# The last part's r and k products in float16 pairs, with scales found on the chip

## The chip, the cores and the metric

The kernel runs on one NeuronCore of one Trainium2 chip. The metric is the device time of the whole launch in microseconds (us), lower is better. Five engines matter: PE (matrix products, with its weight loads shown as PEld), DVE (vector work), ACT (activation functions and copies), POOL (vector work on a slower engine, reductions across partitions) and SP (which issues the DMA transfers). Each takes its own instructions in the order in which the compiled program lists them, and waits at an instruction until what it reads is there.

## The reference

Linear attention on 8 batches of 576 positions, then a feed-forward net behind a Fourier transform, then a gated net (the last part). Only the last part is touched by the change:

```python
def _moe2_ref(x, mu_k, mu_r, w_k, w_v, w_r):
    x_prev = x shifted by one position, zeros at the start of each batch
    xk = mu_k * x + (1.0 - mu_k) * x_prev
    xr = mu_r * x + (1.0 - mu_r) * x_prev
    k = np.maximum(xk @ w_k, 0.0)          # 512 -> 1024
    v = k * k @ w_v                        # 1024 -> 512
    r = 1.0 / (1.0 + np.exp(-(xr @ w_r)))  # 512 -> 512
    return r * v
```

The weights arrive as 64-bit floats. The kernel gets a float32 out of each pair of words on the chip.

## The kernel before

Tokens (8 x 576 = 4608) are cut into 9 blocks of 512. The program has three stretches.

The front (attention, Fourier transform, normalisation, lines 314 to 660) runs as generators `front_x` and `front_y`. The feed-forward main loop (lines 823 to 887) calls them piece by piece through `side()`, four times in each step of a block, so that the front of the later batches lies beside the products of the earlier ones. In the main loop a block has 16 steps; each is 12 products of 512 columns at L846 (first layer, into the PSUM tile `h`) and 12 at L866 (second layer, into four accumulators `acc`), all float16: a float32 number is held as a high and a low float16 part and three products stand for one. ACT writes the high part of the result (`hh`, L851) and DVE the low part (`hl`, L852), two steps ahead of their use.

The last strand (`last_strand`, L804) is called through the same `side()` when the front is used up. It first runs `last_weights` (L668): for each chunk of 128 x 256 weights a DMA into one of three `raw` buffers (L150), three DVE instructions that make a float32 from the two words (L157 to L159), an ACT copy into the high part (L684) and a DVE subtraction for the low part (L685). There are 8 chunks of `w_r`, 16 of `w_k` and 16 of `w_v`, in this order. Then it loads the block's activations (`load_y`) and mixes them (`mix`, L701): per quarter of the features an ACT product (L714), a POOL memset of one column where a batch starts (L717), a DVE multiply-add (L718), an ACT copy to the high part (L719), a DVE subtraction for the low part (L720). For the second and later blocks `mix` is called from the last part's own loop.

The last part (lines 890 to 956) takes the 9 blocks in turn. A block has 48 products for r (L908, four groups of 12, sigmoid by ACT at L909), 96 for k (L919, `mmk`, eight groups of 12), and 96 for v (L934, `mmv`). All three use float32r, a format of 4 bytes, again in high and low parts. Behind each `mmk` ACT takes relu (L923), DVE multiplies by it once more (L924, so k squared), ACT copies the high part (L925) and DVE subtracts (L926). `mmv(f)` uses what `mmk(f)` left two groups earlier. Two PSUM tiles `h` alternate, so `mmk(f+2)` waits until L924 has read the tile of `mmk(f)`.

The compiled order of the instructions is not the order of the source: when the program is built, a planner simulates the engines and moves an instruction forward where its engine would be idle. So the chunks of `last_weights`, which the source places in block 7 of the main loop, run from the end of block 6 on.

Of the kernel before, what the change touches and what calls it, by code (L numbers as in the profile page):

```python
# [22 lines left out]
RAW = 3  # L23
# [18 lines left out]
LEAST = (1.0 + 0x300000 / 2.0 ** 23) * 2.0 ** (0x73 - 127)  # L42
# [3 lines left out]
def net(ctx, tc, q, k, v, w1, w2, mu_k, mu_r, w_k, w_v, w_r, ce_d, se_d, cs_d, ss_d, alt_d, id_d, out):  # L46
    nc = tc.nc
# [4 lines left out]
    FK = w_k.shape[1]  # L52
    NFK = FK // 128
    blocks = [(t, min(512, NT - t)) for t in range(0, NT, 512)]
# [6 lines left out]
    def bank(tag, bufs, shape=(128, 512)):  # L61
        return ps.tile(list(shape), F32, tag=tag, name=tag, bufs=bufs)
# [27 lines left out]
    up = main.enter_context(tc.tile_pool(name="up", bufs=4, side="right"))  # L90
    hp = main.enter_context(tc.tile_pool(name="hp", bufs=1, side="right"))
# [107 lines left out]
    def scales(w):  # L199
# [66 lines left out]
    W = {}  # L266
# [37 lines left out]
    def attention(b):  # L304
        tt = nc.vector.tensor_tensor
        for hf in range(2):
# [14 lines left out]
            m = fw.tile([128, 4, 64], F32, tag="m", name="m")  # L321
            nc.vector.tensor_reduce(out=m, in_=kc.rearrange("p c h d -> p h d c"), axis=AX.X, op=ALU.max)  # L322
            for x in range(2):
                p = slice(64 * x, 64 * x + 64)
                tt(out=m[p, 2 * x:2 * x + 2, :], in0=m[p, 2 * x:2 * x + 2, :], in1=kt[p, 16:18, :], op=ALU.max)
            if b in MAX_PE:
# [4 lines left out]
                mx = wsc[:, 2:6:3, None]  # L331
                nc.vector.tensor_reduce(out=mx[:, :, 0], in_=pt[:, 0:256].rearrange("p (x c) -> p x c", x=2), axis=AX.X, op=ALU.max)
                dg = m.rearrange("p h d -> p (h d)").rearrange("p (x c) -> p x c", x=2)
# [7 lines left out]
            st = fw.tile([128, 2, 18, 1], F32, tag="st", name="st")  # L341
            nc.vector.tensor_reduce(out=st[:, 0, :, 0], in_=qt, axis=AX.X, op=ALU.max)
            beside = nc.gpsimd.tensor_tensor if (b, hf) in POOL_Q else tt
# [322 lines left out]


    back_pools = ExitStack()  # L668
    def last_weights():

        wp = W["pool"] = back_pools.enter_context(tc.tile_pool(name="wp", bufs=1))
        W["mu"] = wp.tile([128, 2, 2, 4], F32, name="mu")
        for x, src in enumerate((mu_k, mu_r)):
            nc.sync.dma_start(out=W["mu"][:, x, 0, :], in_=src)
        nc.vector.tensor_scalar(out=W["mu"][:, :, 1], in0=W["mu"][:, :, 0], scalar1=-1.0, scalar2=1.0, op0=ALU.mult, op1=ALU.add)
        for name, src, nt, n in (("wr", w_r, 4, DM), ("wk", w_k, 4, FK), ("wv", w_v, NFK, DM)):
            h = wp.tile([128, nt, n], F32R, name=name + "h")
            l = wp.tile([128, nt, n], F32R, name=name + "l")
            W[name] = h, l
            for t in range(nt):  # L680
                for c in range(n // 256):
                    cs = slice(256 * c, 256 * c + 256)
                    x = decode(wp, load_weight(wp, src, t, c, RAW))
                    nc.scalar.activation(out=h[:, t, cs], in_=x, func=AF.Copy)  # L684
                    nc.vector.tensor_tensor(out=l[:, t, cs], in0=x, in1=h[:, t, cs].bitcast(F32), op=ALU.subtract)  # L685
                    yield 0


    Y = {}
    X = {}  # L690

    def load_y(i):
        t0, n = blocks[i]
# [4 lines left out]
        else:  # L698
            nc.sync.dma_start(out=y[:, :, 0:n + 1], in_=yT[:, :, t0 - 1:t0 + n].rearrange("t p n -> p t n"))

    def mix(i, w):  # L701

        t0, n = blocks[i]
        y = Y[i]
        mu = W["mu"]
        if w == 1:
            h, l = (up.tile([128, 4, 512], F32R, tag="u", name="x") for _ in range(2))
        else:
            h, l = (hp.tile([128, 4, 512], F32R, tag=x, name="x") for x in ("sq", "d"))
        X[i, w] = h, l  # L710
        aa = hp.tile([128, 2, 512], F32, tag="rs", name="aa")
        for t in range(4):
            a = aa[:, t % 2, 0:n]
            nc.scalar.activation(out=a, in_=y[:, t, 0:n], func=AF.Copy, scale=mu[:, w, 1, t:t + 1])  # L714
            for b, s, m, o in segments(i):
                if s == 0:
                    nc.gpsimd.memset(a[:, o:o + 1], 0.0)  # L717
            nc.vector.scalar_tensor_tensor(out=a, in0=y[:, t, 1:n + 1], scalar=mu[:, w, 0, t:t + 1], in1=a, op0=ALU.mult, op1=ALU.add)  # L718
            nc.scalar.activation(out=h[:, t, 0:n], in_=a, func=AF.Copy)  # L719
            nc.vector.tensor_tensor(out=l[:, t, 0:n], in0=a, in1=h[:, t, 0:n].bitcast(F32), op=ALU.subtract)  # L720
            yield 0


# [164 lines left out]
        side()  # L888


    mu = W["mu"]
    (wkh, wkl), (wvh, wvl), (wrh, wrl) = W["wk"], W["wv"], W["wr"]
    kk = big.tile([128, 2, 4, 512], F32R, tag="w1h", name="kk")
    ke = big.tile([128, 8, 512], F32, tag="w1l", name="ke")
# [2 lines left out]
    for i, (t0, n) in enumerate(blocks):  # L897
        subs = [(o, min(128, n - o)) for o in range(0, n, 128)]
        rh, rl = X.pop((i, 1))
        kh, kl = X.pop((i, 0))  # L900
        acc = [bank(f"acc{x}", 1) for x in range(4)]
        E = ke[:, 0:4, :]
        nxt = iter(())
        for x, (o, m) in enumerate(subs):
            pt = bank("h", 2)
            for t in range(4):
                for a, c in ((rh, wrh), (rh, wrl), (rl, wrh)):
                    mm(out=pt[0:m, :], lhsT=a[:, t, o:o + m], rhs=c[:, t, :], start=(t == 0 and a is rh and c is wrh), stop=(t == 3 and a is rl))  # L908
            nc.scalar.activation(out=E[0:m, x, :], in_=pt[0:m, :], func=AF.Sigmoid)  # L909
        if i + 1 < NB:  # L910
            nxt = mix(i + 1, 1)
        K2 = {}

        def mmk(f):
            pt = bank("h", 2)
            fs = slice(128 * f, 128 * f + 128)
            for t in range(4):
                for a, c in ((wkh, kh), (wkh, kl), (wkl, kh)):
                    mm(out=pt[:, 0:n], lhsT=a[:, t, fs], rhs=c[:, t, 0:n], start=(t == 0 and a is wkh and c is kh), stop=(t == 3 and a is wkl))  # L919
            kr = ke[:, 4 + count[0] % 4, :]  # L920
            h2, l2 = kk[:, 0, count[0] % 4, :], kk[:, 1, count[0] % 4, :]
            count[0] += 1
            nc.scalar.activation(out=kr[:, 0:n], in_=pt[:, 0:n], func=AF.Relu)  # L923
            nc.vector.scalar_tensor_tensor(out=kr[:, 0:n], in0=pt[:, 0:n], scalar=0.0, in1=kr[:, 0:n], op0=ALU.max, op1=ALU.mult)  # L924
            nc.scalar.activation(out=h2[:, 0:n], in_=kr[:, 0:n], func=AF.Copy)  # L925
            nc.vector.tensor_tensor(out=l2[:, 0:n], in0=kr[:, 0:n], in1=h2[:, 0:n].bitcast(F32), op=ALU.subtract)  # L926
            K2[f] = h2, l2

        def mmv(*fs):
            for x, (o, m) in enumerate(subs):  # L930
                for f in fs:
                    h2, l2 = K2[f]
                    for a, c in ((h2, wvh), (h2, wvl), (l2, wvh)):
                        mm(out=acc[x][0:m, :], lhsT=a[:, o:o + m], rhs=c[:, f, :], start=(f == 0 and a is h2 and c is wvh), stop=(f == NFK - 1 and a is l2))  # L934


        lag = 3 if i == NB - 1 else 2
# [131 lines left out]
```

## Time and profile before

| what | value |
|---|---|
| median of three runs | 1605.52 us (1602.82 to 1607.69) |
| the profiled execution's own time | 1604.72 us |
| its span, first to last instruction | 1602.9 us |
| mean granted TensorE clock, as a share of full speed | 0.971 |
| PE busy / PEld busy | 93% / 59% |
| DVE / ACT / POOL busy | 56% / 36% / 10% |

The time of an execution is 1.8 us more than its span. PE's busy share counts modelled ends of pipelined products, so the distance between the starts of successive products says more than a product's duration.

### The profile page before, as it was taken

Reading aid. Unit: us, or ns where it says so; the run is one execution under the profiler, and the core shown is the slowest. Engines: PE = TensorE matmul, PEld = TensorE weight load, DVE = VectorE, ACT = ScalarE, POOL = GpSimd, SP = SyncE. Lnnn points to the kernel's source line nnn. Section 1 sums busy time; section 2 is a strip of 40 time slices with the busy share of each in tenths; the row PEclk is TensorE's granted clock in tenths of the full one; section 3 lists DMA queues with packets and bytes.
Section 4 is the critical chain, followed back from the end, with each engine's and each line's share of the span. In section 5 each row is a group of like instructions: output and inputs, shape, how many; then the busy total and the mean of one; then the engine's idle time right before and its main releaser. Section 6 shows DMA issues by size and latency. Waiting matters only on the chain.

```text
span 1602.9 us, 17944 instructions
## 1 busy us (share of the span) xinstructions
PE 1489.3 (93%) x7072; PEld 945.5 (59%) x7072; DVE 893.8 (56%) x1496; ACT 579.1 (36%) x1010; POOL 164.8 (10%) x174
## 2 busy tenths in 40 slices
PE   4657895899999999999999899999999999999999
PEld 3535443555555555555555344446888888888887
DVE  6899958646657465485454893513344443434432
ACT  4655543333234233242232331313334433433421
POOL 0034422120010110110200210000000000000000
PEclk9778997899999999999999999999999999999999
DMA  9845411101111012021011330101001101100000
GB/s 356 315 134 181 147 58 72 47 32 46 42 46 59 15 47 73 1 73 47 0 53 47 99 119 27 54 0 53 27 27 53 53 16 37 53 27 27 27 27 27
DMA packets 41407, 105.98 MB, mean 66 GB/s; under 512 B 5323, under 2 KB 11628, under 8 KB 40300
## 3 DMA queue, kind: packets, MB, share of 16 engines
q1 hardware_dynamic: 41324, 104.85, 18.6%
q8 instruction: 55, 0.90, 0.2%
q14 instruction: 28, 0.23, 0.0%
HBM read 85.96 MB, written 18.87 MB: 65 GB/s over the span
## 4 chain that ended last, share of the span: by engine, by line
PE 78%; DVE 14%; DMA 3%; issue 2%; ACT 2%; POOL 1%; SPq 0%; DVEq 0%; POOLq 0%; ACTq 0%
PE acc L866 18%; PE h L846 18%; PE acc L934 13%; PE h L919 13%; PE h L908 6%; PE side L495 2%; PE side L515 2%; DMA raw<-in_w_k_dram 1%; PE side L416 1%; PE side L363 1%; DMA raw<-in_w_dram 1%; DVE words L239 1%; DVE m L322 1%; DVE top L197 1%; DVE eo L450 1%
## 5 line engine op out<-in xcount | busy, mean ns | idle before, releaser
L846 PE MATMUL h<-unh,w1h 128*128 128x512 f16 (+1 forms) x608 | 225.3, 371 | 7.3 <-DVE hl L852 4.2
L846 PE MATMUL h<-unh,w1l 128*128 128x512 f16 (+1 forms) x608 | 223.9, 370 | 5.5 <-POOL w1l L257 5.5
L846 PE MATMUL h<-unl,w1h 128*128 128x512 f16 (+1 forms) x608 | 225.0, 370 | 1.2 <-DVE unl L658 1.2
L866 PE MATMUL acc<-hl,w2h 128*128 128x512 f16 x576 | 219.8, 382 | 2.7 <-DVE hl L852 2.7
L866 PE MATMUL acc<-hh,w2l 128*128 128x512 f16 x576 | 219.9, 382 | 0.0
L866 PE MATMUL acc<-hh,w2h 128*128 128x512 f16 x576 | 211.7, 381 | 4.9 <-ACT hh L851 4.9
L846 PEld LDWEIGHTS <-w1h 128*128 128x128 f16 x1216 | 118.3, 99 | 136.8 <-issue 7.8
L852 DVE SCALAR_TENSOR_TENSOR hl<-h,hh 128x512 f16<-128x512 f32 x144 | 98.9, 688 | 179.5 <-ACT hh L851 178.6
L866 PEld LDWEIGHTS <-w2h 128*128 128x128 f16 x1152 | 111.8, 98 | 137.0 <-issue 8.1
L934 PE MATMUL acc<-wvh,kk 128*128 128x512 f32 x576 | 190.6, 395 | 0.0
L919 PE MATMUL h<-x,wkh 128*128 128x512 f32 x576 | 180.8, 395 | 0.0
L851 ACT ACTIVATE hh<-h 128x512 f16<-128x512 f32 x144 | 85.0, 592 | 215.4 <-PE h L846 215.2
L924 DVE SCALAR_TENSOR_TENSOR ke<-h,ke 128x512 f32<-128x512 f32 x72 | 49.7, 690 | 177.5 <-ACT ke L923 177.4
L934 PEld LDWEIGHTS acc<-wvh,kk 128*128 128x128 f32 x576 | 108.1, 188 | 26.3
L919 PEld LDWEIGHTS h<-x,wkh 128*128 128x128 f32 x576 | 108.1, 188 | 26.2
L934 PE MATMUL acc<-wvl,kk 128*128 128x512 f32 x288 | 113.7, 395 | 0.0
L919 PE MATMUL h<-x,wkl 128*128 128x512 f32 x288 | 113.7, 395 | 0.0
L923 ACT ACTIVATE ke<-h 128x512 f32<-128x512 f32 x72 | 42.9, 596 | 175.6 <-PE h L919 175.5
L846 PEld LDWEIGHTS <-w1l 128*128 128x128 f16 x608 | 59.7, 98 | 72.4 <-POOL w1l L257 7.9
L866 PEld LDWEIGHTS <-w2l 128*128 128x128 f16 x576 | 56.6, 98 | 67.5 <-issue 5.3
L908 PE MATMUL h<-wrh,x 128*128 128x512 f32 x288 | 92.1, 396 | 0.0
L720 DVE TENSOR_TENSOR x<-aa,x 128x512 fp32r<-128x512 f32 x72 | 47.8, 688 | 72.6 <-PE h L908 62.4
(309 smaller groups left out, 2253.3 us busy)
## 6 DMA issues: line engine op xcount, KB each, us to landing
raw<-in_w_dram SPq DMA_DIRECT2D x22, 512.0 KB, 3.8
vt<-in_v_dram SPq DMA_DIRECT2D x16, 650.0 KB, 5.2
kt<-in_k_dram SPq DMA_DIRECT2D x16, 576.0 KB, 3.9
qt<-in_q_dram SPq DMA_DIRECT2D x16, 576.0 KB, 4.0
out_dram<-oo SPq DMA_DIRECT2D x36, 256.0 KB, 2.1
y<-yT SPq DMA_DIRECT2D x8, 1026.0 KB, 5.1
w2h<-in_w_dram SPq DMA_DIRECT2D x8, 1024.0 KB, 5.1
w2l<-in_w_dram SPq DMA_DIRECT2D x8, 1024.0 KB, 7.1
```

Of the source, the lines that this page charges most:

```text
L495: mm(out=pt, lhsT=a[:, e, g, js], rhs=c[:, g, :], start=first, stop=(e == 1 and g == 1 and a is el))
L515: mm(out=pt, lhsT=a[:, i, cols], rhs=c[:, i, :], start=(i == 0 and c is ch and a is yh), stop=False)
L720: nc.vector.tensor_tensor(out=l[:, t, 0:n], in0=a, in1=h[:, t, 0:n].bitcast(F32), op=ALU.subtract)
L846: mm(out=pt[:, o:o + m], lhsT=a[:, t, fs], rhs=c[:, t, o:o + m], start=(t == 0 and a is w1h and c is xh), stop=(t == 3 and a is w1l))
L851: nc.scalar.activation(out=hh[:, 0:n], in_=pt[:, 0:n], func=AF.Relu)
L852: nc.vector.scalar_tensor_tensor(out=hl[:, 0:n], in0=pt[:, 0:n], scalar=0.0, in1=hh[:, 0:n], op0=ALU.max, op1=ALU.subtract)
L866: mm(out=acc[x][:, 0:n], lhsT=a[:, f, xs], rhs=c[:, 0:n], start=(f == 0 and a is w2h and c is hh), stop=(f == NF - 1 and a is w2l))
L908: mm(out=pt[0:m, :], lhsT=a[:, t, o:o + m], rhs=c[:, t, :], start=(t == 0 and a is rh and c is wrh), stop=(t == 3 and a is rl))
L919: mm(out=pt[:, 0:n], lhsT=a[:, t, fs], rhs=c[:, t, 0:n], start=(t == 0 and a is wkh and c is kh), stop=(t == 3 and a is wkl))
L923: nc.scalar.activation(out=kr[:, 0:n], in_=pt[:, 0:n], func=AF.Relu)
L924: nc.vector.scalar_tensor_tensor(out=kr[:, 0:n], in0=pt[:, 0:n], scalar=0.0, in1=kr[:, 0:n], op0=ALU.max, op1=ALU.mult)
L934: mm(out=acc[x][0:m, :], lhsT=a[:, o:o + m], rhs=c[:, f, :], start=(f == 0 and a is h2 and c is wvh), stop=(f == NFK - 1 and a is l2))
```

## The change

`last_weights` first finds two bounds. For `w_r` and `w_k` (24 chunks) it loads each chunk, takes the absolute value of the words' upper 16 bits by ACT into a bfloat16 tile, and the maximum by DVE; then the maximum across partitions by POOL. From this come powers of two. Only then are the weights loaded (again, for `w_r` and `w_k`) and cut, in the order `w_v`, `w_r`, `w_k`; r's and k's are scaled and held as two float16 parts, v's stay float32r. For each block of tokens `bound` finds the largest absolute value of the block (a DVE reduction over 4 x 513 numbers per partition, then POOL across partitions), and six small DVE instructions make the block's scales. The mixing factors carry the scale, the mixed activations are float16 pairs, and the sigmoid and the relu undo the scales through their scale operand. The memset at batch starts goes from POOL to DVE. The number of products, their shapes and their order are the same.

```diff
+        top = wp.tile([128, 4], F32, name="top")
+        am = wp.tile([128, 2, 16], F32, name="am")
+        nc.gpsimd.memset(am, 0.0)
...
+        for w, (name, src, nt, n) in enumerate(plan[0:2]):
+            for t in range(nt):
+                for c in range(n // 256):
+                    raw = load_weight(wp, src, t, c, RAW)
+                    hw = wp.tile([128, 256], BF16, tag="hw", name="hw", bufs=2)
+                    a = t * (n // 256) + c
+                    nc.scalar.activation(out=hw, in_=raw[:, :, 1:2].bitcast(BF16)[:, :, 1], func=AF.Abs)
+                    ts(out=hw, in0=hw, scalar1=0.0, scalar2=None, op0=ALU.max, op1=ALU.max, accum_out=am[:, w, a:a + 1])
+                    yield 0
+        nc.vector.tensor_reduce(out=top[:, 0:2], in_=am, axis=AX.X, op=ALU.max)
+        nc.gpsimd.partition_all_reduce(out_ap=top[:, 0:3], in_ap=top[:, 0:3], channels=128, reduce_op=bass_isa.ReduceOp.max)
...
+        for name, src, nt, n in (plan[2], plan[0], plan[1]):
+            f16 = name != "wv"
...
+            h = wp.tile([128, nt, n], F16 if f16 else F32R, name=name + "h")
+            l = wp.tile([128, nt, n], F16 if f16 else F32R, name=name + "l")
...
+                    if f16:
+                        s = pw[:, 2 + (name == "wk"):3 + (name == "wk")]
+                        nc.scalar.activation(out=h[:, t, cs], in_=x, func=AF.Copy, scale=s)
+                        nc.vector.scalar_tensor_tensor(out=l[:, t, cs], in0=x, scalar=s, in1=h[:, t, cs], op0=ALU.mult, op1=ALU.subtract)
...
+    def bound(i):
...
+        nc.vector.tensor_reduce(out=z[:, 0:1], in_=Y[i][:, :, 0:n + 1], axis=AX.XY, op=ALU.max, apply_absolute_value=True)
+        nc.gpsimd.partition_all_reduce(out_ap=z[:, 0:1], in_ap=z[:, 0:1], channels=128, reduce_op=bass_isa.ReduceOp.max)
+        yield 0
+        zi = z.bitcast(U32)
+        ts(out=z[:, 1:2], in0=z[:, 0:1], scalar1=W["top"][:, 2:3], scalar2=LEAST, op0=ALU.mult, op1=ALU.max)
...
     def mix(i, w):
...
+        if i not in SC:
+            yield from bound(i)
+        mu = SC[i][1]
         if w == 1:
-            h, l = (up.tile([128, 4, 512], F32R, tag="u", name="x") for _ in range(2))
+            h, l = (up.tile([128, 4, 512], F16, tag="u", name="x") for _ in range(2))
...
-                    nc.gpsimd.memset(a[:, o:o + 1], 0.0)
+                    nc.vector.memset(a[:, o:o + 1], 0.0)
...
-            nc.scalar.activation(out=E[0:m, x, :], in_=pt[0:m, :], func=AF.Sigmoid)
+            nc.scalar.activation(out=E[0:m, x, :], in_=pt[0:m, :], func=AF.Sigmoid, scale=z[0:m, 3:4])
...
-            nc.scalar.activation(out=kr[:, 0:n], in_=pt[:, 0:n], func=AF.Relu)
+            nc.scalar.activation(out=kr[:, 0:n], in_=pt[:, 0:n], func=AF.Relu, scale=z[:, 5:6])
```

## Rows read from the trace of the kernel before

**Rows 1.** Busy by stretch: length, each engine's busy us (instructions), granted clock, DMA.

```profile
880.00:940.00 60.00, 51.69 (x220) 22.23 (x218) 54.22 (x115) 19.73 (x42) 14.83 (x6) 0.94 0.34 108
867.00:972.00 105.00, 96.69 (x428) 42.64 (x426) 93.28 (x212) 37.03 (x77) 16.29 (x9) 0.97 0.35 111
972.00:1095.00 123.00, 123.00 (x572) 55.73 (x570) 33.91 (x54) 25.75 (x42) 0.79 (x8) 1.00 0.05 18
1095.00:1603.00 508.00, 504.15 (x2163) 405.39 (x2161) 204.60 (x309) 184.56 (x306) 5.32 (x54) 1.00 0.10 36
```

**Rows 2.** The chain that ended last: start us, us, engine, tile, line, products.

```profile
1004.87 7.77 PE acc L866 x36
...
1095.51 11.19 PE h L908 x48
1106.71 8.40 PE h L919 x36
```

**Rows 3.** A group of PE: count, busy us, mean ns of one, idle before.

```profile
L919 PE MATMUL h<-x,wkh 128*128 128x512 f32 x576 | 180.8, 395 | 0.0
```

**Rows 4.** Whom PE waited for, 820 to 1000 us: total us, times, longest.

```profile
PE acc L866 <- ACT hh L851: 4.5, 2, 2.5
PE acc L866 <- DVE hl L852: 2.7, 2, 2.3
```

**Rows 5.** ACT in order of time, before PE's longest wait (914.6).

```profile
913.67 0.42 ACT L684 ACTIVATE wkh<-dec 128x256 fp32r<-128x256 f32 x1 [2.92 <-DVE dec L159]
913.99 0.58 ACT L851 ACTIVATE hh<-h 128x512 f16<-128x512 f32 x1
```

**Rows 6.** PE in order of time, a float32r product among float16 ones.

```profile
941.84 0.38 PE L846 MATMUL h<-unl,w1h 128*128 128x512 f16 x1
941.87 0.58 PE L581 MATMUL side<-hl,onesr 128*128 128x512 f32 x1
942.29 0.39 PE L846 MATMUL h<-unh,w1l 128*128 128x512 f16 x1
```

**Rows 7.** Groups that cut the weights (L158), and searched the main loop's (L196, L197).

```profile
L158 DVE SCALAR_TENSOR_TENSOR dec<-raw,dec 128x256 uint32<-128x256 uint32 x40 | 19.5, 494 | 0.1
...
L197 DVE TENSOR_SCALAR_CACHE_REDUCE top<-top 128x512 bf16<-128x512 bf16 x32 | 20.6, 680 | 0.2
...
L197 DVE DVE_READ_ACCUMULATOR top<-top 128x1 f32 x32 | 2.6, 82 | 0.0
...
L196 ACT ACTIVATE top<-w2l 128x512 bf16<-128x512 bf16 x16 | 9.7, 650 | 0.0
```

**Rows 8.** DMA issues: count, KB each, median us from issue to landing.

```profile
raw<-in_w_k_dram SPq DMA_DIRECT2D x16, 256.0 KB, 3.2
```

**Rows 9.** DVE in order of time: the last weight chunk, then block 0's mixing.

```profile
971.51 0.43 DVE L685 TENSOR_TENSOR wvl<-dec,wvh 128x256 fp32r<-128x256 f32 x1 [0.48 <-ACT wvh L684]
...
1017.33 1.29 DVE L720 TENSOR_TENSOR x<-aa,x 128x512 fp32r<-128x512 f32 x2 [0.74 <-DMA yT<-u]
...
1034.44 1.41 DVE L718 SCALAR_TENSOR_TENSOR aa<-y,mu,aa 128x512 f32<-128x512 f32 x2 [2.32 <-POOL aa L717]
```

**Rows 10.** POOL in order of time: two of the ten maxima across partitions.

```profile
262.69 1.08 POOL L338 PARTITION_ALL_REDUCE m<-m  x1 [6.02 <-issue]
...
739.85 1.06 POOL L338 PARTITION_ALL_REDUCE m<-m  x1 [23.62 <-DVE m L325]
```

**Rows 11.** Groups nearest to the added instructions, and the mixing lines.

```profile
L718 DVE SCALAR_TENSOR_TENSOR aa<-y,mu,aa 128x512 f32<-128x512 f32 x72 | 51.0, 747 | 15.2 <-POOL aa L717 14.2 <-ACT aa L714 1.0
...
L322 DVE TENSOR_REDUCE m<-kt 128x256 f32<-128x1024 f32 x16 | 31.0, 1936 | 11.9 <-DMA kt<-in_k_dram 11.8
L354 DVE TENSOR_REDUCE st<-qt 128x18 f32<-128x1152 f32 x16 | 21.6, 1351 | 11.8 <-ACT qt L345 11.8
...
L458 DVE MEMSET eo<- 1x289 f32 x3 | 0.9, 299 | 0.0
...
L714 ACT ACTIVATE aa<-y,mu 128x512 f32<-128x512 f32 x72 | 48.2, 716 | 13.9 <-DVE x L720 7.8 <-DVE d L644 3.9 <-DMA y<-yT 2.1
```

More of the change, by code (lines that the diff above doesn't have):

```diff
@@ L671, in last_weights @@
         wp = W["pool"] = back_pools.enter_context(tc.tile_pool(name="wp", bufs=1))
+        ts = nc.vector.tensor_scalar
         W["mu"] = wp.tile([128, 2, 2, 4], F32, name="mu")
@@ L674, in last_weights @@
             nc.sync.dma_start(out=W["mu"][:, x, 0, :], in_=src)
[L675 to L678, printed above, removed]
+        ts(out=W["mu"][:, :, 1], in0=W["mu"][:, :, 0], scalar1=-1.0, scalar2=1.0, op0=ALU.mult, op1=ALU.add)
@@ new lines, in last_weights @@
+        top = wp.tile([128, 4], F32, name="top")
+        am = wp.tile([128, 2, 16], F32, name="am")
+        nc.gpsimd.memset(am, 0.0)
+        ab = wp.tile([128, 2, 2, 4], F32, name="ab")
+        nc.vector.scalar_tensor_tensor(out=ab, in0=W["mu"], scalar=-1.0, in1=W["mu"], op0=ALU.mult, op1=ALU.max)
+        nc.vector.tensor_tensor(out=ab[:, :, 0], in0=ab[:, :, 0], in1=ab[:, :, 1], op=ALU.add)
+        nc.vector.tensor_reduce(out=top[:, 2:3], in_=ab[:, :, 0], axis=AX.XY, op=ALU.max)
+        yield 0
@@ new lines, in last_weights @@
+        plan = (("wr", w_r, 4, DM), ("wk", w_k, 4, FK), ("wv", w_v, NFK, DM))
+        for w, (name, src, nt, n) in enumerate(plan[0:2]):
[7 more added lines that the diff above has]
+                    yield 0
@@ new lines, in last_weights @@
+        nc.vector.tensor_reduce(out=top[:, 0:2], in_=am, axis=AX.X, op=ALU.max)
+        nc.gpsimd.partition_all_reduce(out_ap=top[:, 0:3], in_ap=top[:, 0:3], channels=128, reduce_op=bass_isa.ReduceOp.max)
+        yield 0
+        W["top"] = top
+        pw = W["pw"] = wp.tile([128, 4], F32, name="pw")
+        scaled = False
+        for name, src, nt, n in (plan[2], plan[0], plan[1]):
+            f16 = name != "wv"
+            if f16 and not scaled:
+                m, inv, big_ = pw[:, 0:2], pw[:, 2:4], top[:, 0:2]
+                mi, ii, bi = m.bitcast(U32), inv.bitcast(U32), big_.bitcast(U32)
+                ts(out=big_, in0=big_, scalar1=LEAST, scalar2=None, op0=ALU.max)
+                ts(out=mi, in0=bi, scalar1=3, scalar2=0x3F800000, op0=ALU.logical_shift_left, op1=ALU.bitwise_and)
+                nc.vector.scalar_tensor_tensor(out=mi, in0=bi, scalar=0x40000000, in1=mi, op0=ALU.bitwise_and, op1=ALU.bitwise_or)
+                ts(out=ii, in0=mi, scalar1=0x7F800000, scalar2=None, op0=ALU.bitwise_xor)
+                ts(out=inv, in0=inv, scalar1=2.0 ** 11, scalar2=None, op0=ALU.mult)
+                scaled = True
+            h = wp.tile([128, nt, n], F16 if f16 else F32R, name=name + "h")
+            l = wp.tile([128, nt, n], F16 if f16 else F32R, name=name + "l")
@@ L683, in last_weights @@
                     x = decode(wp, load_weight(wp, src, t, c, RAW))
-                    nc.scalar.activation(out=h[:, t, cs], in_=x, func=AF.Copy)
-                    nc.vector.tensor_tensor(out=l[:, t, cs], in0=x, in1=h[:, t, cs].bitcast(F32), op=ALU.subtract)
+                    if f16:
+                        s = pw[:, 2 + (name == "wk"):3 + (name == "wk")]
+                        nc.scalar.activation(out=h[:, t, cs], in_=x, func=AF.Copy, scale=s)
+                        nc.vector.scalar_tensor_tensor(out=l[:, t, cs], in0=x, scalar=s, in1=h[:, t, cs], op0=ALU.mult, op1=ALU.subtract)
+                    else:
+                        nc.scalar.activation(out=h[:, t, cs], in_=x, func=AF.Copy)
+                        nc.vector.tensor_tensor(out=l[:, t, cs], in0=x, in1=h[:, t, cs].bitcast(F32), op=ALU.subtract)
                     yield 0
@@ L690, in net @@
     X = {}
+    SC = {}
     def load_y(i):
@@ L699, in load_y @@
             nc.sync.dma_start(out=y[:, :, 0:n + 1], in_=yT[:, :, t0 - 1:t0 + n].rearrange("t p n -> p t n"))
+    def bound(i):
+        n = blocks[i][1]
+        ts = nc.vector.tensor_scalar
+        z = W["pool"].tile([128, 6], F32, tag="z", name="z", bufs=3)
+        ms = W["pool"].tile([128, 2, 2, 4], F32, tag="ms", name="ms", bufs=3)
+        SC[i] = z, ms
+        nc.vector.tensor_reduce(out=z[:, 0:1], in_=Y[i][:, :, 0:n + 1], axis=AX.XY, op=ALU.max, apply_absolute_value=True)
+        nc.gpsimd.partition_all_reduce(out_ap=z[:, 0:1], in_ap=z[:, 0:1], channels=128, reduce_op=bass_isa.ReduceOp.max)
+        yield 0
+        zi = z.bitcast(U32)
+        ts(out=z[:, 1:2], in0=z[:, 0:1], scalar1=W["top"][:, 2:3], scalar2=LEAST, op0=ALU.mult, op1=ALU.max)
+        ts(out=zi[:, 1:2], in0=zi[:, 1:2], scalar1=0x7F800000, scalar2=None, op0=ALU.bitwise_and)
+        ts(out=zi[:, 2:3], in0=zi[:, 1:2], scalar1=0x7F800000, scalar2=None, op0=ALU.bitwise_xor)
+        ts(out=ms, in0=W["mu"], scalar1=z[:, 2:3], scalar2=2.0 ** 12, op0=ALU.mult, op1=ALU.mult)
+        ts(out=z[:, 3:5], in0=W["pw"][:, 0:2], scalar1=z[:, 1:2], scalar2=2.0 ** -25, op0=ALU.mult, op1=ALU.mult)
+        nc.vector.tensor_tensor(out=z[:, 5:6], in0=z[:, 4:5], in1=z[:, 4:5], op=ALU.mult)
+        yield 0
     def mix(i, w):
@@ L704, in mix @@
         y = Y[i]
-        mu = W["mu"]
+        if i not in SC:
+            yield from bound(i)
+        mu = SC[i][1]
         if w == 1:
-            h, l = (up.tile([128, 4, 512], F32R, tag="u", name="x") for _ in range(2))
+            h, l = (up.tile([128, 4, 512], F16, tag="u", name="x") for _ in range(2))
         else:
-            h, l = (hp.tile([128, 4, 512], F32R, tag=x, name="x") for x in ("sq", "d"))
+            h, l = (hp.tile([128, 4, 512], F16, tag=x, name="x") for x in ("sq", "d"))
         X[i, w] = h, l
@@ L716, in mix @@
                 if s == 0:
-                    nc.gpsimd.memset(a[:, o:o + 1], 0.0)
+                    nc.vector.memset(a[:, o:o + 1], 0.0)
             nc.vector.scalar_tensor_tensor(out=a, in0=y[:, t, 1:n + 1], scalar=mu[:, w, 0, t:t + 1], in1=a, op0=ALU.mult, op1=ALU.add)
             nc.scalar.activation(out=h[:, t, 0:n], in_=a, func=AF.Copy)
-            nc.vector.tensor_tensor(out=l[:, t, 0:n], in0=a, in1=h[:, t, 0:n].bitcast(F32), op=ALU.subtract)
+            nc.vector.tensor_tensor(out=l[:, t, 0:n], in0=a, in1=h[:, t, 0:n], op=ALU.subtract)
             yield 0
@@ L888, in net @@
         side()
-    mu = W["mu"]
     (wkh, wkl), (wvh, wvl), (wrh, wrl) = W["wk"], W["wv"], W["wr"]
@@ L900, in net @@
         kh, kl = X.pop((i, 0))
+        z = SC[i][0]
         acc = [bank(f"acc{x}", 1) for x in range(4)]
```

## The prediction

> **What bounds the kernel now.** I read the busy time by stretch first. From 1095 us to the end, the last part, PE is busy for 504 of 508 us at full clock, while DVE has work for 205 and ACT for 185 of them; from 972 to 1095 PE is busy throughout. Only from 867 to 972, where the weights of the last part are cut, is DVE nearly full (93.3 of 105), and there PE loses time: 51.7 busy of 60 us between 880 and 940, at a mean granted clock of 0.94 [rows 1]. So in the last part the spacing of PE's products is the time, and in that one earlier stretch DVE is.
>
> How far apart the products are is read from the chain, which there runs through PE alone: 48 products of r take 11.19 us and 36 of k take 8.40, that is 0.2331 and 0.2333 us for a float32r product of 512 columns; 36 float16 products of the main loop take 7.77, 0.2158 each [rows 2]. The page's durations (0.395 for L919, and 0.0 idle before 576 of them) are longer than these distances because one product begins before the one ahead has ended [rows 3]; I don't use them.
>
> The loss in the earlier stretch has two parts. 60 - 51.7 = 8.3 us are idle, and of them 7.2 are four waits for `hh` and `hl`, what ACT and DVE write behind the first layer [rows 4]. The clock at 0.94 costs up to 0.06 x 60 = 3.6 us more: after the longest waits it falls from 2.4 GHz to 1.2 for a while. Together up to 11.9 us. Why `hh` is late is seen on ACT: it stands right behind a weight copy (L684) that waited 2.92 us for DVE's decoding [rows 5]. The instruction order is fixed, so whoever stands behind a late chunk is late too.
>
> **The change part by part.**
>
> *The products.* r has 9 x 48 = 432 and k 9 x 96 = 864 of them; they keep their shapes and order and become float16. By the main loop's distance they gain 432 x (0.2331 - 0.2158) = 7.5 us and 864 x (0.2333 - 0.2158) = 15.1, together 22.6 us, all of it on PE, which sets the end. v's 864 stay as they are. In the new k and v stretch the two formats alternate by groups. What a switch costs is bounded by a place where a float32r product stands between two float16 ones: from 941.84 to 942.29 there are two products, 0.45 us, and 0.2158 + 0.2333 is 0.449 [rows 6]. So a switch costs nothing, and the distance belongs to the format and not to the place in the kernel.
>
> By the Trainium skill, page "TensorE: Matmul & The Clock Gate", section "Back-to-back issue gap", the distance is the columns over 2.4 GHz plus 2.5 ns, 216 ns for 512, with no word on the format. That agrees with the float16 row and not with the float32r ones, 0.233; by it the change of format would bring nothing, and it is a rival below.
>
> *The search for the largest weight.* 24 chunks more, each a DMA, an ACT instruction and a DVE maximum with its accumulator read. The main loop's search took 680 + 82 ns on DVE and 650 on ACT for 512 columns [rows 7]; these have 256, so between half and all of it: on DVE 0.42 to 0.76 us, on ACT 0.33 to 0.65. I take the lower ends, since the time of both goes with the columns: 24 x 0.42 = 10 us of DVE and 24 x 0.33 = 8 of ACT. A DMA of a chunk lands 3.2 us after its issue [rows 8], and with three buffers a chunk can come every (3.2 + 0.4) / 3 = 1.2 us at best. SP issues these in its one queue, and the writes of `yT` and the loads of `y` stand behind them.
>
> Two things follow for the stretch from 867. For a gain: the chunks that come first now need 0.42 us of DVE in place of four instructions of which L158 alone took 0.49 [rows 7]; the expensive decoding moves behind the start of block 7, to where DVE has 34 us of work in 123 [rows 1]. At best all 11.9 us of PE's loss go. For a loss: ACT now waits for the DMA itself, with `hh` behind it in its queue, and DVE's maximum waits for ACT, with `hl` behind it. If each added chunk costs PE as much as one of the 40 does now, 11.9 / 40 = 0.30 us, that is 7 us more. I take 0, between -12 and +7, because the two act on the same queues and I see no row that ranks them.
>
> *How late the weights are.* 40 chunks took the 105 us from 867 to 972, 2.6 each; 24 more at that pace end 63 us later than the last one did, at 971.9 + 63 = 1035. Block 0's mixing took from 1017 to 1036, some 19 us [rows 9], and could then end by 1054. The last part starts at 1095, so 41 us are left: nothing. If the cover were gone (a pace of 2.6 + 41/24 = 4.3 us a chunk), each us would count in full.
>
> *The scale of each block.* On DVE a maximum over 4 x 513 = 2052 numbers per partition: at L354's 1.17 ns a number 2.4 us, at L322's 1.89 (strided) 3.9 [rows 11]; I take 2.4, as the numbers lie in a row. Six small instructions, each at most the 0.3 of the 289-column memset [rows 11], make 1.8. So 4 to 6 us a block beside 205/9 = 23 of 56 [rows 1]: hidden. The POOL maximum takes 1.1 us. When POOL had done other work right before, 6.02 us passed first in which it waited for nothing that is shown (three of ten times); otherwise it started when DVE delivered [rows 10].
>
> The wait that is added is DVE's, for POOL. Behind it on DVE stand L924 and L926 of the running k group; PE needs L924's reading of the `h` tile before the next group but one. Once v has begun, a k and a v group lie between, 12 x 0.2158 + 12 x 0.2333 = 5.4 us, of which ACT and DVE themselves need some 1.3: 4.1 us of slack, against 1.1 to 1.5 of wait. Nothing is paid.
>
> *The rest.* 64 memsets go from POOL to DVE, at most 0.3 us each, 19 us over the last part; in exchange L718 no longer waits for POOL, 14.2 us in all [rows 11]. The relu and sigmoid with a scale operand take at most the 0.716 of L714 [rows 11], 108 x 0.716 = 77 us where ACT has 185 of 508. The high and low parts cost the same instructions as before. All hidden, so 0; without the cover the memsets and the scale of 9 blocks would be 19 + 9 x 5 = 64 us, which is the work that DVE's idle 303 us have to take.
>
> *Sum.* The profiled execution took 1604.7 us (span 1602.9 and 1.8 around it), 0.8 below the median 1605.5. 1604.7 - 22.6 + 0 = 1582.1 us.
>
> **The rivals.**
>
> A, the forecast: PE sets the last part, the front changes by -8 to +7: 1574 to 1589.
>
> B, the front gets worse than that: ACT's waits for the raw chunks fall on PE with 0.3 to 0.8 us for each of 24, +7 to +19: 1589 to 1601. For it speaks that ACT's queue has `hh` right behind weight work [rows 5]; against it that `hh` is made two steps, 5.2 us, ahead of its use.
>
> C, the decoding is so well spread that PE's whole loss there goes: -8 to -12, 1570 to 1574.
>
> D, slower: DVE waits for POOL in each of the last part's blocks. Price: 6.0 us before POOL starts, 1.1 for the maximum and a handover, together 7.5, less the slack of 4.1, is 3.4 us; and while the first two k groups follow each other without v the slack is only 2.6 - 1.3 = 1.3, so 6.2. Eight blocks at 3.4 to 6.2 are 27 to 50 us: 1609 to 1632. It decides from 22.6 / 8 = 2.8 us a block on. For it: the 6.02 us stand in the trace. Against it: they came where POOL had just done other work, and in the last part POOL would do nothing but these maxima, since the memsets leave it; also, the planner can put the maximum long before its use. The Trainium skill, page "GPSIMD Engine Reference", section "2.1 Instruction dispatch", has about 6 us for the first call to a freshly loaded POOL program; the row agrees, and by that rule it is paid only where POOL's program changes.
>
> E, the gain doesn't come: r's and k's products keep 0.233 us. It would have to be something that all products of the last part share. Against it is the float32r product in the main loop, which needs the same 0.233 there [rows 6]. With the front at 0: 1605.
>
> **How the numbers follow.** A 0.72, B 0.10, C 0.06, D 0.06, E 0.06. Likeliest: A at 1582. The range takes all of A and most of C and half of B (to 1595): 1571 to 1595, some 0.8. About 0.3%, 4.8 us, is what a measurement of this kernel can tell from no change. Faster (under 1600.7) are A, B and C, 0.88; within it E and little else, 0.06; slower D, 0.06.
>
> **What would show it right or wrong.** In the chain, 48 products of r in 10.4 us and 12 of k in 2.6, with v's 12 still in 2.8; the last part from its first r product to the end some 23 us shorter. Between 867 and 1095, PE's idle time beside the 8.3 us of before, and the waits of L866 for `hh` and `hl`; the last chunk of weights before 1060. In the last part, no wait of PE on L924, and DVE's waits for POOL under 2 us. The prediction is wrong if PE has waits in the last part, if the last part starts later than before by over 10 us, or if the distance of the float16 products there is not the main loop's.

## The result and the profile after

| | before | changed |
|---|---|---|
| median | 1604.99 us (4 runs) | 1590.54 us (4 runs, 1589.88 to 1592.45) |
| the profiled execution: time / span | 1604.72 / 1602.9 us | 1591.17 / 1589.4 us |
| last Fourier step to first product of r | 229.4 us | 235.6 us |
| first product of r to the end | 507.7 us | 485.2 us |

The ratio is 0.991 (95% interval 0.9896 to 0.9924): 14.5 us less, where 23 were forecast. The two stretches are cut at two places that both kernels have: the start of the last L538 on DVE and the first r product. The instructions of each stand in the views by line (count, shortest/median/longest ns, first and last start); first the kernel before, then the changed one:

```profile
L538 DVE TENSOR_TENSOR u<-u,sd x8: 748/750/752, 71.3 to 865.8; 128x574 f32<-128x574 f32 x8
L908 PE MATMUL h<-wrh,x x288: 390/395/581, 1095.2 to 1554.0; 128*128 128x512 f32 x144
```

```profile
L538 DVE TENSOR_TENSOR u<-u,sd x8: 749/750/752, 73.9 to 868.6; 128x574 f32<-128x574 f32 x8
L975 PE MATMUL h<-wrh,x x288: 378/379/392, 1104.2 to 1542.1; 128*128 128x512 f16 x144
```

1095.2 - 865.8 = 229.4 and 1602.9 - 1095.2 = 507.7; 1104.2 - 868.6 = 235.6 and 1589.4 - 1104.2 = 485.2. So the last part is 22.5 us shorter, the stretch where its weights are cut 6.2 us longer. Up to the last L538 the order of the instructions on all five engines is the same in both, and the 2.8 us between 865.8 and 868.6 are no effect of the change: 2.3 of them are there when the first block's output is written (241.8 and 244.1 us), and over all kernels below that point lies anywhere from 864.0 to 868.7.

The chain in the last part (start us, us, engine, tile, line, products). First v's products in the kernel before, whose r and k stand in [rows 2], then the changed kernel:

```profile
1115.10 2.80 PE acc L934 x12
```

```profile
1104.39 10.36 PE h L975 x48
1114.75 7.77 PE h L986 x36
1122.52 2.79 PE acc L1001 x12
1125.32 2.61 PE h L986 x12
1133.35 2.79 PE acc L1001 x12
...
1144.12 2.77 PE acc L1001 x12
```

r's 48 products take 10.36 us for 11.19, k's 36 take 7.77 for 8.40: 0.2158 each, the main loop's distance. v's 12 in float32r stay at 2.77 to 2.79, for 2.80 before.

Busy time by stretch (columns as in [rows 1]) and whom PE waited for between 820 and 1104 us [rows 4]:

```profile
880.00:940.00 60.00, 48.78 (x206) 21.00 (x205) 45.52 (x126) 23.86 (x50) 8.84 (x6) 0.94 0.47 149
869.00:1003.00 134.00, 120.17 (x533) 52.94 (x532) 107.56 (x282) 51.27 (x106) 14.99 (x11) 0.97 0.42 134
1003.00:1104.00 101.00, 101.00 (x469) 45.80 (x468) 34.91 (x66) 23.18 (x38) 0.38 (x1) 1.00 0.06 22
1104.00:1590.00 486.00, 481.58 (x2162) 284.23 (x2160) 224.97 (x412) 192.73 (x306) 4.42 (x7) 1.00 0.10 37
```

```profile
PE h L913 <- DVE hl L919: 6.4, 5, 2.9
PE acc L933 <- ACT hh L918: 3.6, 3, 2.2
PE acc L933 <- DVE hl L919: 2.6, 2, 2.0
PE side L581 <- ACT hl L579: 1.2, 1, 1.2
```

PE is idle for 11.2 us between 880 and 940, where it was for 8.3, and some more up to 1003, when the last weight is cut: 13.8 us in all in these waits, 5.5 more than the kernel before and most of the 6.2, at the same granted clock of 0.94 between 880 and 940. DVE, though, is less busy there than before, 45.5 of 60 for 54.2. What DVE and ACT do instead is in the groups of ACT between 867 and 1004 us, and in DVE and PE in order of time:

```profile
L694 ACT ACTIVATE hw<-raw 128x256 bf16<-128x256 bf16 x24 | 10.3, 432 | 17.5 <-DMA raw<-in_w_k_dram 10.9 <-DMA raw<-in_w_r_dram 6.4 <-DVE hw L695 0.2
```

```profile
904.43 0.29 DVE L157 TENSOR_SCALAR dec<-raw 128x256 uint32<-128x256 uint32 x1 [0.90 <-DMA raw<-in_w_v_dram]
...
907.81 0.68 DVE L919 SCALAR_TENSOR_TENSOR hl<-h,hh 128x512 f16<-128x512 f32 x1
```

```profile
908.54 0.59 PE L913 MATMUL h<-unh,w1h 128*128 128x512 f16 x1 [2.91 <-DVE hl L919]
```

ACT's 24 searching instructions wait 17.5 us, nearly all for chunks to land. DVE waits for ACT in turn, 14.3 us in all at the search's maxima (L695). A late chunk shifts everything behind it in both queues. `hl`, whose `hh` was written by 905.1, starts at 907.81, and PE has waited 2.91 us for the PSUM tile it frees. In that case the wait for a landing was 0.90 us; from 904.43 on DVE had no gap, and `hl` stood behind 3.4 us of the search, of decoding, of the scales and of the normalisation.

### The profile page after: what moved, and what is told of

Read it like the earlier page. It is cut to its first block, busy times and chain, and to the rows that moved or that the text cites. A ratio compares the mean times of both kernels' runs of the same rounds, so it can differ in the third digit from the quotient of the medians.

```text
span 1589.4 us, 18119 instructions
## 1 busy us (share of the span) xinstructions
PE 1470.3 (93%) x7072; PEld 827.7 (52%) x7072; DVE 926.5 (58%) x1680; ACT 598.1 (38%) x1034; POOL 163.6 (10%) x121
## 4 chain that ended last, share of the span: by engine, by line
PE 74%; DVE 15%; DMA 5%; issue 2%; ACT 2%; POOL 2%; SPq 0%; DVEq 0%; ACTq 0%; POOLq 0%
PE acc L933 17%; PE h L913 17%; PE acc L1001 13%; PE h L986 12%; PE h L975 6%; DMA raw<-in_w_k_dram 3%; PE side L495 2%; PE side L515 2%; DMA raw<-in_w_dram 1%; PE side L416 1%; DVE words L239 1%; PE side L363 1%; DVE hl L919 1%; DVE dec L159 1%; DVE m L322 1%
## 5 line engine op out<-in xcount | busy, mean ns | idle before, releaser
L1001 PE MATMUL acc<-wvh,kk 128*128 128x512 f32 x576 | 202.9, 416 | 0.0
L986 PE MATMUL h<-x,wkh 128*128 128x512 f16 x576 | 173.0, 380 | 0.0
L986 PE MATMUL h<-x,wkl 128*128 128x512 f16 x288 | 109.2, 379 | 0.0
L990 ACT ACTIVATE ke<-h,z 128x512 f32<-128x512 f32 x72 | 49.2, 683 | 140.8 <-PE h L986 140.8
L986 PEld LDWEIGHTS <-wkh 128*128 128x128 f16 x576 | 52.7, 98 | 70.5 <-issue 14.0
L975 PE MATMUL h<-wrh,x 128*128 128x512 f16 x288 | 88.6, 380 | 0.0
L787 DVE TENSOR_TENSOR x<-aa,x 128x512 f16<-128x512 f32 x72 | 47.9, 686 | 61.0 <-PE h L975 52.4
```

## The experiments

Each ratio is to the kernel before on the same chip, where its median was 1605.0 to 1606.9 us. "Stretch" is from the last Fourier step to the first r product, "last part" from there to the end, both of the one profiled execution. How far a stretch can be trusted is seen on kernels with the same instructions in the same order on every engine: e8 has 237.7 us for the changed kernel's 235.6, e7 and e12 have 228.6 and 229.5 for 229.4 before. A difference of 2 us between two stretches shows nothing.

| kernel | median us | ratio to before (95%) | stretch | last part |
|---|---|---|---|---|
| before (first profile) | 1604.99 | 1 | 229.4 | 507.7 |
| changed | 1590.54 | 0.991 (0.9896 to 0.9924) | 235.6 | 485.2 |
| e1_no_search | 1583.20 | 0.9856 (0.9841 to 0.9870) | 228.9 | 485.2 |
| e2_raw8 | 1584.14 | 0.9859 (0.9844 to 0.9873) | 230.1 | 485.0 |
| e3_no_switch | 1592.14 | 0.9905 (0.9888 to 0.9922) | 239.4 | 485.1 |
| e4_search_alone | 1595.40 | 0.9932 (0.9917 to 0.9947) | 233.1 | 493.8 |
| e5_behind | 1588.39 | 0.9897 (0.9874 to 0.9920) | 234.0 | 485.0 |
| e6_before_behind | 1596.68 | 0.9948 (0.9930 to 0.9967) | 221.0 | 507.7 |
| e7_pad_before | 1591.36 | 0.9913 (0.9892 to 0.9935) | 228.6 | 493.8 |
| e8_pad_after | 1588.32 | 0.9893 (0.9867 to 0.9918) | 237.7 | 483.6 |
| e9_all | 1577.12 | 0.9812 (0.9792 to 0.9831) | 223.0 | 483.6 |
| e10_raw8_pad | 1582.71 | 0.9848 (0.9828 to 0.9867) | 230.3 | 483.6 |
| e11_before_best | 1584.59 | 0.9861 (0.9846 to 0.9876) | 221.4 | 493.7 |
| e12_pad64 | 1603.73 | 0.9981 (0.9971 to 0.9992) | 229.5 | 505.0 |

### Where the 6 us in the front come from

**Without the search.**

```diff
-        nc.gpsimd.memset(am, 0.0)
+        nc.gpsimd.memset(am, 1.625)
...
-        for w, (name, src, nt, n) in enumerate(plan[0:2]):
...
```

> The changed kernel without the search: the 24 chunks are not loaded and not looked through, the largest weight is set to a constant (1.625, the upper bits of 0.25); the maxima across partitions on POOL stay. The stretch from the last Fourier step (start of the last L538) to the first product of r is 229.4 us in the kernel before and 235.6 in the changed one. Theory S (the 24 search chunks stand in ACT's and DVE's queues ahead of the main loop's hh and hl): the stretch falls to 228 to 230, the time by about 6 us to 1584 or 1585. Rival P (POOL changes its program four times between the normalisation's sums and the maxima, 6 us each): stays at 234 to 236, time 1590.

The stretch fell to 228.9 us. The search costs 6.7 us there, all that the front had lost and a little more. This is what theory S gave, but the run does not rule out rival P. The two maxima stayed, yet without the search they stand side by side on POOL, and its program changes twice there instead of four times:

```profile
877.51 0.38 POOL L745 PARTITION_ALL_REDUCE z<-z  x1 [7.15 <-issue]
877.81 0.45 POOL L689 PARTITION_ALL_REDUCE top<-top  x1
```

**Without the changes of POOL's program.**

```diff
-        nc.gpsimd.partition_all_reduce(out_ap=top[:, 0:3], in_ap=top[:, 0:3], channels=128, reduce_op=bass_isa.ReduceOp.max)
...
-        nc.gpsimd.partition_all_reduce(out_ap=z[:, 0:1], in_ap=z[:, 0:1], channels=128, reduce_op=bass_isa.ReduceOp.max)
+        if i > 0:
+            nc.gpsimd.partition_all_reduce(out_ap=z[:, 0:1], in_ap=z[:, 0:1], channels=128, reduce_op=bass_isa.ReduceOp.max)
```

> The changed kernel without the maximum across partitions of the weights and without that of block 0 (each partition keeps its own; blocks 1 to 8 as they are), so that POOL needs no other program before the normalisation's last sums are done. Theory S: the stretch from the last Fourier step to the first product of r stays at 234 to 236 us, time 1590. Rival P: it falls to 229 to 231, time about 1585.

The kernel leaves out two of the maxima, so its scales are not valid and only its time is of use. The stretch is 239.4 us, neither what S expected nor what P did, and not shorter; so the changes that are gone were not what the front had lost to. PE's waits in this kernel, 860 to 1200 us, are again for what stands in DVE's queue:

```profile
PE h L913 <- DVE hl L919: 12.0, 5, 3.2
PE acc L933 <- DVE u L951: 2.0, 1, 2.0
PE side L581 <- ACT hl L579: 1.5, 1, 1.5
```

The planner orders the queues anew for every kernel whose instructions change. The profiled execution was the slowest of four (1594.7 us, median 1592.1), and by the intervals of the table this kernel can't be told from the changed one.

**Eight buffers for the raw chunks.**

```diff
-RAW = 3
+RAW = 8
```

> The changed kernel with eight raw buffers in place of three. If what the search and the cutting cost PE is the wait for landing chunks in queues of fixed order: the stretch from 235.6 to 227 to 231 us, time 1582 to 1586, and ACT's and DVE's waits for raw chunks nearly gone. If it is the work itself on DVE and ACT: stays at 234 to 236, time 1590.

230.1 us: 5.5 us go, though the work is the same. Up to 885 us the order on DVE and ACT is the changed kernel's; behind that the planner made another one. The searching line's waits in this kernel:

```profile
L694 ACT ACTIVATE hw<-raw x24: 413/432/441, 871.2 to 895.1; 128x256 bf16<-128x256 bf16 x24
...
  DMA raw<-in_w_r_dram: 5.1, 7
  DVE hw L695: 1.5, 5
  DMA raw<-in_w_k_dram: 0.2, 1
```

ACT waits 5.3 us for landing chunks in place of 17.3. POOL's program still changes four times, since the two maxima lie apart with elementwise work between them:

```profile
879.92 0.38 POOL L754 PARTITION_ALL_REDUCE z<-z  x1 [10.80 <-DVE hw L695]
...
898.20 0.38 POOL L698 PARTITION_ALL_REDUCE top<-top  x1 [6.13 <-DVE dec L159]
```

The loss is gone with them in place, and it stayed without them (e3): rival P falls, and theory S holds. The eight buffers serve the cutting too: DVE's waits for its chunks, 8.4 us in the changed kernel and 8.2 in the kernel before, are gone. So the stretch is long mostly by waits for landings in queues of fixed order, and little by the work. How much of the 5.5 us is the search's and how much the cutting's is not shown, since the kernel before was not run with eight buffers.

**The search alone, in the kernel before.** Nobody reads its result; it uses the `dec` buffers.

```diff
+        am = wp.tile([128, 2, 16], F32, name="am")
+        plan = (("wr", w_r, 4, DM), ("wk", w_k, 4, FK), ("wv", w_v, NFK, DM))
+        for w, (name, src, nt, n) in enumerate(plan[0:2]):
...
+                    nc.scalar.activation(out=hw, in_=raw[:, :, 1:2].bitcast(BF16)[:, :, 1], func=AF.Abs)
+                    nc.vector.tensor_scalar(out=hw, in0=hw, scalar1=0.0, scalar2=None, op0=ALU.max, op1=ALU.max, accum_out=am[:, w, a:a + 1])
```

> The kernel before, with the 24 search chunks added ahead of the cutting (its result is used by nobody, no maximum across partitions, all products float32r, order of the weights as before). Theory S: the stretch from the last Fourier step to the first product of r grows from 229.4 to about 235 us, time about 1611. Rival P: 229 to 230, time 1605. The last part keeps its 507.7 us in both.

The stretch grew by 3.7 us, less than the 6 that S gave, but the kernel got 0.7% faster, which neither theory had: its last part, with the same products in the same order, took 493.8 us for 507.7. This led to the experiments on placement below.

**The weight work behind block 7, in the changed kernel and in the kernel before.** The DVE and ACT instructions of the search and the decoding (in the kernel before only the decoding) are queued behind the float16 halves of block 7.

```diff
+        if i == NB - 2:
+            mark("cut", mv, ma)
...
+                    with behind("cut"):
+                        x = decode(wp, raw)
```

> The changed kernel with the search and the decoding of the weights queued on ACT and DVE behind the float16 halves of block 7 (the last instructions that block 7 of the main loop needs). The same work, only later. If weight work put ahead of the normalisation of block 7 is what PE loses to between 880 and 940 us: the stretch from the last Fourier step to the first product of r falls from 235.6 to 220 to 228 us, unless the weights are then late for the last part; time 1578 to 1584. If the work costs the same wherever it lies: 234 to 236, time 1590.

> The kernel before with the decoding of its weights queued behind the float16 halves of block 7 in the same way. If that is what PE loses to there: the stretch from 229.4 to 219 to 224 us, time 1595 to 1600; the last part keeps its 507.7. If not: 229.4, time 1605.

In the kernel before, the chunks are loaded from 867.6 us on. That is the middle of block 6, whose products run from 819.8 to 926.7, and not its end, as the description of that kernel has it. With the decoding queued behind, the stretch fell by 8.4 us to 221.0. Its busy time by stretch, and then one of PE's waits between 820 and 1104 us:

```profile
880.00:940.00 60.00, 60.00 (x279) 27.25 (x278) 43.41 (x84) 18.28 (x35) 10.02 (x5) 1.00 0.20 65
940.00:1000.00 60.00, 56.17 (x259) 25.00 (x257) 49.79 (x133) 21.54 (x48) 0.32 (x2) 1.00 0.37 116
```

```profile
PE h L850 <- DVE hl L856: 3.8, 5, 1.6
```

PE's loss between 880 and 940 is gone, clock included, and 3.8 us come up later: it was the weight work pulled ahead of block 7's normalisation that cost it. In the changed kernel, where 220 to 228 us were expected, the same move gave 234.0, a gain of 1.6 us that is within the scatter. There the waits moved, into block 7 and the beginning of block 8 (busy time by stretch):

```profile
900.00:940.00 40.00, 38.31 (x177) 17.27 (x175) 20.42 (x60) 15.89 (x34) 3.62 (x2) 1.00 0.50 148
940.00:1000.00 60.00, 54.20 (x240) 23.82 (x240) 52.74 (x156) 22.84 (x49) 0.44 (x1) 0.97 0.47 143
1000.00:1060.00 60.00, 55.30 (x246) 24.46 (x246) 42.69 (x102) 22.61 (x41) 0.37 (x1) 0.97 0.25 79
```

### Where the tiles lie

**A pad of 128 bytes in the kernel before.**

```diff
         W["mu"] = wp.tile([128, 2, 2, 4], F32, name="mu")
+        wp.tile([128, 32], F32, name="pad")
```

> The kernel before with nothing but an unused tile of 128 bytes per partition ahead of the weights of the last part, which shifts all their tiles by 128 bytes; the instructions and their order are the same. In the kernel with the search added to float32r products the last part took 493.8 us in place of 507.7, 0.2267 us a product in place of 0.2333, and its weights lay 128 bytes further on. Theory A (where the weights lie relative to the activations sets the distance of float32r products): last part 494 us, time about 1591 to 1592. Rival W (it was something else in that kernel, the search or the later cutting): last part 507.7, time 1605.

The last part took 493.8 us, as theory A had it, and rival W falls; the chain there, against [rows 2]:

```profile
1106.71 8.16 PE h L920 x36
1114.87 2.72 PE acc L935 x12
1117.59 2.72 PE h L920 x12
```

0.2267 us a float32r product in k and v alike, for 0.2333. A tile that nobody uses brings 13.9 us, and the kernel is as fast as the changed one (ratio 0.9913 against 0.991). By the addresses of the compiled program the weights lay at 192 modulo 512 before and lie at 320 now; the activations that they meet lie at 320 in all these kernels. Of a product's two operands PE loads one ahead (PEld) and streams the other through: in r and v the weights are streamed, in k they are loaded. All three got faster, so the place of the streamed operand alone does not decide, and that of the loaded one alone doesn't either. That the two must lie alike, as theory A says, is the likely reading, but no run moved the activations.

**A pad of 64 bytes.** The same edit with `[128, 16]`.

> The kernel before with 64 unused bytes in place of 128, so that the weights lie 64 bytes off the activations' address modulo 512. If only the offset of 0 is fast: the last part stays near 507.7 us; if the distance grows with the offset: between 494 and 507; if 64-byte steps do not matter: 494. Time 1591 to 1605 accordingly.

505.0 us: in between, and not the same for all products. k's, where the moved weights are loaded, come down a little; r's and v's, where they are streamed, stay:

```profile
1108.50 8.25 PE h L920 x36
1116.76 2.80 PE acc L935 x12
...
1154.12 10.03 PE h L909 x43
```

**Pads in the changed kernel.** 384 bytes ahead of the high part of `w_v`, 256 between its parts.

```diff
+            if name == "wv":
+                wp.tile([128, 96], F32, name="pad0")
             h = wp.tile([128, nt, n], F16 if f16 else F32R, name=name + "h")
+            if name == "wv":
+                wp.tile([128, 64], F32, name="pad1")
             l = wp.tile([128, nt, n], F16 if f16 else F32R, name=name + "l")
```

> The changed kernel with two unused tiles: 384 bytes ahead of the high part of w_v and 256 between its high and low part, so that the high part lies at the same address modulo 512 as the activations it meets, and the low part 256 bytes off; w_r and w_k (float16) shift too. Theory A: v's products come down from 0.231 to 0.233 us to about 0.227 with the high part, and the low part shows whether 256 bytes off is as good; last part from 485.2 to about 481 us; r's and k's stay at 0.2158. Rival W: all as in the changed kernel. The front stays as in the changed kernel, 234 to 236 us, in both.

The last part fell by 1.6 us, not by 4: neither reading. Float16 products kept their distance (k's 36 still take 7.77, though `w_k` moved by 640 bytes), but v's groups of 12 came only to 0.229 to 0.231. The stretch, expected at 234 to 236, was 237.7 with the instructions in the same order.

**All three together, and two of them.** e9 is the version queued behind, with eight buffers and the 384 bytes; e10 is the changed kernel with eight buffers and the 384 bytes.

> The changed kernel with the search and the decoding queued behind block 7's halves, with eight raw buffers, and with 384 unused bytes ahead of w_v, so that both its parts lie at the activations' address modulo 512. If landing chunks were what kept the version queued behind at 234.0 us: stretch from the last Fourier step to the first product of r 222 to 228; if DVE's work in block 7 itself was: 232 to 235. Last part by placement 481 (v at 0.227 us a product), otherwise 485. Time 1572 to 1579 by both first readings, 1588 by both second ones.

> The changed kernel with eight raw buffers and 384 unused bytes ahead of w_v, in the order of the changed kernel. Stretch as with eight buffers alone, 229 to 231 us; last part by placement 481, otherwise 485. Time about 1580 or 1584.

e9's stretch is 223.0 us: with enough buffers the move behind block 7 gains here too, so it was landings, not DVE's work, that kept e5 at 234.0. e10's is that of eight buffers alone. In both the last part is 483.6, between the two readings and the same as in e8, where the low part of `w_v` lay 256 bytes off: a shift by 256 bytes makes no difference here. With both parts of `w_v` at the activations' address modulo 512, v's groups of 12 still take 0.229 to 0.231 a product, though the same residues gave 0.2267 where all products were float32r:

```profile
1109.65 0.58 PE L1008 MATMUL acc<-wvh,kk 128*128 128x512 f32 x1
1110.07 0.40 PE L1008 MATMUL acc<-wvl,kk 128*128 128x512 f32 x1
1110.31 0.40 PE L1008 MATMUL acc<-wvh,kk 128*128 128x512 f32 x1
1110.54 0.40 PE L1008 MATMUL acc<-wvl,kk 128*128 128x512 f32 x1
1110.78 0.39 PE L1008 MATMUL acc<-wvh,kk 128*128 128x512 f32 x1
1111.00 0.39 PE L1008 MATMUL acc<-wvl,kk 128*128 128x512 f32 x1
```

This is e9's PE in order of time: within one group the distances are 0.23 to 0.24 at first and 0.22 to 0.23 later. What comes after 12 products is seen where v's groups follow each other, in e9's chain:

```profile
1131.52 2.77 PE acc L1008 x12
...
1136.89 5.49 PE acc L1008 x24
...
1560.55 10.94 PE acc L1008 x48
```

Each of these stands behind float16 products. The first 12 take 2.77 us; the next 12 take 5.49 - 2.77 = 2.72 and the next 36 take 8.17, that is 0.2267 and 0.2269 each. So with the operands placed well a float32r product does reach 0.2267 here, but only some ten products after the change of format, and the change costs 0.05 us a group. In the changed kernel, where they lie badly, nothing of this is seen: a run of 24 takes 5.58 us, twice 2.79. Why the products behind a change are slower stays open.

**The kernel before with the pad and the weight work behind.**

> The kernel before, all float32r, with the 128 unused bytes and its decoding queued behind block 7's halves. If the two gains are independent: stretch 221 us, last part 494, time about 1582; if they are the same gain in two ways: 1591 or more. It tells what is left of the change's gain against float32r products that lie well.

221.4 and 493.7 us: the two gains add up, and the kernel with float32r products alone takes 1584.6 us, less than the changed one. Against this, float16 is worth 493.7 - 483.6 = 10.1 us of the last part, and e9, the fastest here, is 7.5 us ahead of it. The distances alone would give 1296 x (0.2267 - 0.2158) = 14.1; of the 4 us between, some 60 groups of v behind float16 products at 0.05 make about 3 (an estimate from e9's chain).

## Why the prediction was right, and where its terms were off

The direction and the range held, and case A's mechanism for the last part too: PE has no waits there, and its products alone set the time. But 1590.5 us lies above A's own 1574 to 1589, in the lower part of B's range.

- *The products, -22.6 us.* Measured -22.5. Distances of 10.36/48 and 7.77/36 were those of the main loop, and v's groups of 12 next to float16 ones took 2.77 to 2.79 for 2.80: in this kernel changing the format from group to group cost nothing, as said; with v placed well it costs 0.05 us a group (e9). The sentence that the distance belongs to the format and not to the place in the kernel was half wrong. It belongs to where the operands lie as well: 8.6 us of the 22.5, 1296 x (0.2333 - 0.2267), come from a bad place that float32r had and that 128 bytes of padding remove (e7). The one float32r product in [rows 6] that I held against it showed one place only. The sum came out because the 0.2333 was read from the very products that were changed; that they lay badly was not known, and the reason given for the term was lucky to that extent. By the Trainium skill's page "TensorE: Matmul & The Clock Gate", section "Back-to-back issue gap", a product of 512 columns by itself takes 216 ns and one in a steady stream 131, with no word on the format. The runs agree with 216 for float16; float32r took 227 to 233 ns, and 131 was seen in no run. The prediction used the 216 as the distance in a stream.
- *The front, 0, between -12 and +7.* This is the term that was mis-sized: it was +6.2, of which the search is 6.7 (e1). I had written that no row ranks the gain against the loss, and took the middle. The gain did not come. The cutting was to move behind the start of block 7, to where DVE is idle; it ran from 904 to 1003 us, and the idle stretch stayed idle (34.9 of 101 us busy from 1003 on). Though DVE has less to do between 880 and 940, PE's idle time there rose. The loss came almost at its bound, 0.30 us a chunk by that reckoning and 6.7 / 24 = 0.28 measured, and for the reason given there, ACT's own wait for the DMA with `hh` behind it and DVE's behind ACT. The work of a chunk was sized near enough: 0.43 us on ACT for 0.33 and 0.50 on DVE for 0.42. With eight buffers the stretch is 1.2 us longer than without the search at three (e2, e1). The row that should have decided was there: a landing of 3.2 us over three buffers against 0.4 us of work a chunk means that the search waits for most of its time.
- *The weights' arrival.* Estimated by 1035, measured 1003; no product waited for a weight.
- *The scales of each block.* The maximum on DVE took 2.29 us (2.4 said), the POOL maximum 0.38 to 0.71 (1.1), and DVE's wait for it shows as 0.6 us once. Rival D needed a change of POOL's program in the last part, and there was none.
- *The memsets on DVE.* 0.06 us each, below the bound of 0.3; L785 no longer waits for POOL.
- *Scatter.* The 2.8 us at the last L538, most of them from the first 240 us, were in no term; they are less than the 4.8 us that the prediction gave as what a measurement can tell from no change.

The sum was 9.1 us low for the profiled execution (1591.2 for 1582.1): 6.2 from the front and 2.8 from this scatter. C, D and E did not happen. The measured +6.2 lies at the edge that divided A from B, so the time stayed inside the range by its width and not because the front was understood.

## What to carry to other kernels

Work that is hidden in an average can still stand ahead of the critical instruction in a queue of fixed order: look at what waits for a DMA in that queue, and give it more buffers or put it behind. Before a format is credited with a gain, shift one operand of the slower format by a few times 64 bytes and look at the distance between its products; here a pad brought as much as the whole change. A gain per product that is read from one stage's trace carries over only if the operands lie alike.

## What the runs showed of the hardware

- The distance between successive float32r products of 512 columns was 0.2267 us or 0.2333 at full clock, for the same program, depending on a shift of the weights by 128 bytes (e7); with 64 bytes it was 0.229 for k and 0.2333 for r and v (e12). In the slow case the weights' address was 128 bytes below the activations' modulo 512, in the fast one equal; 256 bytes off was as good as equal for v's low part (e8 against e9). The weight loads' durations, 188 ns, were the same in both. float16 products took 0.2158 in each of the three places tried. What causes it was not found.
- Behind float16 products a float32r product with well placed operands came down to 0.2267 us only after some ten of its kind: 2.77 us for the first 12, 8.17 for the next 36 (e9).
- POOL changes its program between elementwise work and maxima across partitions (the trace of the kernel before has 12 MODIFY_POOL_CONFIG at L338), and in [rows 10] 6.02 us pass there with no wait shown. In the changed kernel the maxima over the weights and over the first block stand between such elementwise work from 860 to 950 us, and taking them out gained nothing (e3).
